# Block-sparse attention with an eight-expert router: rows of the late expert tiles turned by VectorE instead of TensorE, and one addition moved ahead in a queue

## The chip, the core and the metric

One of the eight cores of a Trainium2 chip runs the whole program. The metric is the device time of one execution in microseconds (us). Four compute engines matter: TensorE (PE in the profile; PEld is its weight load), VectorE (DVE), ScalarE (ACT) and GpSimd (POOL); SyncE (SP) issues most DMAs, GpSimd the indirect ones. Each engine works through its own queue of instructions in order and waits on semaphores where it needs the work of another.

## The reference

All data is float32. The attention has 4 sequences of 768 positions, 8 heads of 64 features, and blocks of 32 positions; the mask `mask` is set by the neighbouring, first, last and sampled blocks.

```python
scores = scale * np.matmul(q, k.transpose(0, 1, 3, 2))
scores = np.where(mask, scores, -1000000000.0)
attn = softmax(scores)
x = np.matmul(attn, v)              # then laid out as 3072 rows of 512 features

xn, en = x / |x|, expert_emb / |expert_emb|
logits = xn @ en.T / tau            # 8 experts
expert_idx = argmax(logits); gate_w = softmax(logits)[expert_idx]
for e in range(8):                  # w1[e]: 512 x 1024, w2[e]: 1024 x 512
    mask = expert_idx == e
    h = np.maximum(x[mask] @ w1[e], 0.0)
    out[mask] = gate_w[mask, None] * (h @ w2[e])
```

## The kernel before

**Attention.** A unit is 128 keys against 384 queries (half a sequence) for a pair of heads; six units make a half pair, and there are 32 half pairs. `score_fast` makes the products of keys and queries (line L358, tile `sc`) and their exponentials on ScalarE (L361, tile `e`). `attend_fast` sums the exponentials over the six units on VectorE (`esum`, L374 and L376) and multiplies by the values into one PSUM accumulator, `av` (L379), of which there is only one buffer. After the sixth unit ScalarE copies one bank of `av` (`part`, L383) and VectorE adds the other bank to it (`at`, L385); then `av` is free for the next half pair. `settle` turns `at` back to rows with TensorE (L407, L414) and divides, into `x`. Between units other work for VectorE is put in: `turn_blocks` turns the 32x32 blocks of the next pair's keys and queries (L274, `kt` and `qt`), and routing and dispatch of earlier sequences run in steps at fixed units. Steps of this kind are traced in a block `issue_after(...)`, which keeps each of their instructions behind a named instruction of the same engine.

**Routing.** `route` finds for each row the expert and the gate, stores the gate as the 513th element of the row, and SP writes the rows to DRAM: `x_dram` for all sequences, `x_early` for the first two.

**Dispatch and experts.** Five early tiles of 128 rows, each of a single expert, are cut from the first two sequences (`slot_e`), while the last sequences are still in attention. The remaining rows are ranked once all are known (`dispatch_late`, `fill_slots`), which gives `slot_l`: for each late tile and each of its 128 places the number of a row. Of 24 late tiles at most, 19 always run and the others only if they are needed (a branch each); in this execution 20 do. Two of the late tiles are mixed: two experts with 64 rows each (`mixed_tile`), placed among the others by `ORDER`.

For tile i, `expert_tile` does

- `fetch`: GpSimd gathers the rows of a later tile from DRAM into one of four buffers `xg` (L785), and SP loads the next expert's `w1` and `w2`, 2048 KB each, into a ring of three (L807). The program asks for the rows of tile i + 2; the scheduler that orders the instructions puts the gather ahead of the scatter before it, so in the compiled order the rows of tile i + 3 are gathered at the start of late tile i;
- 32 products `hp` = w1 by the turned rows `xgt` (L845), in two halves; ScalarE applies the ReLU to the first half (L848), VectorE to the second (L852);
- `prepare(i + 1)`: TensorE turns the next tile's rows with four transposes (L830, tile `xg_ps`), and VectorE copies them to `xgt` (L832);
- 8 products `yp` = h by w2 (L858);
- `finish`: VectorE multiplies by the gate (L866, tile `y`, of which there are two buffers) and GpSimd scatters the rows to the output (L867).

A product in float32 appears in the profile as two matmuls. In a mixed tile the products hold the rows as weights (L886, L906), and `h` is turned back with eight transposes (L898), between whose two halves the next tile is prepared. At the end of the program a count of good denominators decides whether an exact second version has to run; it does not here.

Of the kernel before, what the change touches and what calls it, by code (L numbers as in the profile page):

```python
# [42 lines left out]
for _mixed in range(MIX):  # L43
    ORDER.insert(6 * (_mixed + 1), _mixed)
XW = DM + 1
SCALE = 1.0 / float(D) ** 0.5
# [279 lines left out]
def attend(k, u):  # L326
    nc = k.nc
    h, c = u // NC, u % NC
    g, hh = h // 2, h % 2
    b = g // NPAIR  # L330
    et, v = k.ets.pop(u), k.vs[g]
    if c == 0:
        k.av = two_banks(k, "av")[:, 0, 0:NC * D].rearrange("p (c e) -> p c e", e=D)
    for kc in range(NC):
        nc.tensor.matmul(k.av[:, c, :], lhsT=et[:, kc * P:(kc + 1) * P], rhs=v[:, hh, kc, :],
                         start=(kc == 0), stop=(kc == NC - 1))
    if c == NC - 1:
        if h % H == 0:
            k.x[b] = k.xp.tile([P, NC, XW], F32, name="x", tag="x")
# [3 lines left out]
        at = (h % H) * D  # L343
        nc.vector.tensor_tensor(out=k.x[b][:, :, at:at + D], in0=k.av,
                                in1=den.unsqueeze(2).broadcast_to([P, NC, D]), op=ALU.mult)
# [19 lines left out]
def attend_fast(k, u):  # L365
# [15 lines left out]
    if kc == NC - 1:  # L381
        part = k.sp.tile([P, HALF], F32, name="part", tag="part")
        nc.scalar.copy(out=part, in_=k.av[:, 1, 0:HALF])  # L383
        at = k.sp.tile([P, HALF], F32, name="at", tag="at")
        nc.vector.tensor_tensor(out=at, in0=k.av[:, 0, 0:HALF], in1=part, op=ALU.add)  # L385
        k.done[u // NC] = (at, k.esum)


def settle(k, w):
# [5 lines left out]
    if w % (2 * NPAIR) == 0:  # L395
        k.x[b] = k.xp.tile([P, NC, XW], F32, name="x", tag="x")
        k.nsq[b] = k.xp.tile([P, NC, NPAIR], F32, name="nsq", tag="nsq")
# [11 lines left out]
    for t in range(NQ):  # L409
# [14 lines left out]
    nc.vector.tensor_tensor(  # L424
        out=k.x[b][:, chunks, j * P:(j + 1) * P].rearrange("p t (h d) -> p t h d", h=2),
        in0=rows[:, :, :, 0:D], in1=inv.unsqueeze(3).broadcast_to([P, NQ, 2, D]), op=ALU.mult)
# [4 lines left out]
def squares(k, w):  # L431
# [3 lines left out]
    chunks = slice(qh * NQ, (qh + 1) * NQ)  # L435
    x = k.x[b][:, chunks, j * P:(j + 1) * P]
    sq = k.sp.tile([P, NQ, P], F32, name="sq", tag="sq", bufs=1)
# [9 lines left out]
def last_squares(k, w):  # L447

    b, j, qh = w // (2 * NPAIR), w // 2 % NPAIR, w % 2
    for c in range(qh * NQ, (qh + 1) * NQ):  # L450
        sq = k.sp.tile([P, P], F32, name="sq_l", tag="sq_l")
        k.nc.scalar.activation(sq, k.x[b][:, c, j * P:(j + 1) * P], ACT.Square,
                               accum_out=k.nsq[b][:, c, j:j + 1])
# [20 lines left out]
def logits(k, x):  # L474
    nc, p = k.nc, k.rp
    lg = two_banks(k, "lg")[:, 0, 0:NC * E].rearrange("p (c e) -> p c e", e=E)
    for c2 in range(0, NC, 2):
        ps = k.big.tile([P, 2 * ND, P], F32, name="xt_ps", tag="big")
        for i in range(2 * ND):
            c, d = c2 + i // ND, i % ND  # L480
            nc.tensor.transpose(ps[:, i, :], x[:, c, d * P:(d + 1) * P], k.ident)
        xt = p.tile([P, 2 * ND, P], F32, name="xt")
# [8 lines left out]
def route(k, b):  # L491
# [3 lines left out]
    if k.exact:  # L495
        for c in range(NC):
            sq = p.tile([P, DM], F32, name="sq")
            nc.scalar.activation(sq, x[:, c, 0:DM], ACT.Square, accum_out=nrm[:, c:c + 1])
    else:
# [29 lines left out]
    nc.vector.reduce_max(out=m, in_=pick, axis=AX.X)  # L529
    nc.vector.tensor_tensor(out=oh, in0=pick, in1=wide(m), op=ALU.is_equal)  # L530
    yield
# [3 lines left out]
    for w in (4, 2):  # L535
        nc.gpsimd.tensor_tensor(out=ex[:, :, 0:w], in0=ex[:, :, 0:w], in1=ex[:, :, w:2 * w], op=ALU.add)
    gate = x[:, :, DM:XW]
    nc.gpsimd.tensor_tensor(out=gate, in0=ex[:, :, 0:1], in1=ex[:, :, 1:2], op=ALU.add)
    nc.gpsimd.tensor_scalar(out=gate, in0=gate, scalar1=1e-9, scalar2=None, op0=ALU.add)
    yield  # L540
    nc.vector.reciprocal(out=gate, in_=gate)
    yield
    drams = (k.x_early, k.x_dram) if b < EARLY else (k.x_dram,)
    for dram in drams:
        for c in range(NC):
            nc.sync.dma_start(out=dram[b * S:(b + 1) * S, :].rearrange("(c p) w -> p c w", c=NC)[:, c], in_=x[:, c])
            yield
# [91 lines left out]

def fill_slots(k, lanes, val, nt, tiles, name):  # L640

    nc, p = k.nc, k.dp
    ps = two_banks(k, "slot_ps")[:, 0, 0:2 * tiles]
    for t in range(nt):
# [46 lines left out]
def dispatch_late(k):  # L691
# [63 lines left out]
    yield  # L755
    k.slots.append(fill_slots(k, k.lanes, val, NT, NL, "slot_l"))
    yield
# [18 lines left out]
def fetch_rows(k, i):  # L776

    late = int(i >= NE)
    x = ring(k, "xg", i, 4, k.wp, [P, XW])
    t = ORDER[i - NE] if late else i  # L780
    slot = k.slots[late][:, t:t + 1]
    with ExitStack() as order:
        if k.squared is not None and not late:
            order.enter_context(k.tc.issue_after(k.squared))
        k.nc.gpsimd.indirect_dma_start(  # L785
            out=x[:, :], out_offset=None, in_=(k.x_dram if late else k.x_early)[:, :],
            in_offset=bass.IndirectOffsetOnAxis(ap=slot, axis=0),
            bounds_check=N if late else EARLY * S - 1, oob_is_err=False,
        )
    k.rows[i] = x, slot  # L790


def fetch_weights(k, i, at, pieces=1):
# [28 lines left out]
def prepare(k, i):  # L822

    x = k.rows[i][0]
    if i == 0:
        ps = two_banks(k, "first")[:, 0].rearrange("p (d t) -> p d t", d=ND)
    else:
        ps = ring(k, "xg_ps", i, 1, k.eps, [P, ND, P])
    for d in range(ND):
        k.nc.tensor.transpose(ps[:, d, :], x[:, d * P:(d + 1) * P], k.ident)  # L830
    k.turned_rows[i] = ring(k, "xgt", i, 2, k.wp, [P, ND, P])
    k.nc.vector.tensor_copy(out=k.turned_rows[i], in_=ps)  # L832


def expert_tile(k, i, meanwhile=None):
    nc = k.nc
    ((w1, w2),), (x, slot) = k.weights.pop(i), k.rows.pop(i)
    xt = k.turned_rows.pop(i)
    h = ring(k, "h", i, 2, k.wp2, [P, NF, P])
    half = NF // 2  # L840
    for f0 in (0, half):
# [9 lines left out]
        else:  # L851
            nc.vector.tensor_scalar(out=h[:, half:NF], in0=hp, scalar1=0.0, scalar2=None, op0=ALU.max)  # L852

# [3 lines left out]
    for f in range(NF):  # L857
        nc.tensor.matmul(yp, lhsT=h[:, f, :], rhs=w2[:, f, :], start=(f == 0), stop=(f == NF - 1))  # L858
    finish(k, i, yp, x, slot)


def finish(k, i, yp, x, slot):

    nc = k.nc
    y = ring(k, "y", i, 2, k.wp2, [P, DM])
    nc.vector.tensor_scalar(out=y, in0=yp, scalar1=x[:, DM:XW], scalar2=None, op0=ALU.mult)  # L866
    nc.gpsimd.indirect_dma_start(  # L867
# [5 lines left out]
def mixed_tile(k, i):  # L873


    nc = k.nc
    weights, (x, slot) = k.weights.pop(i), k.rows.pop(i)
    xt = k.turned_rows.pop(i)
    half = NF // 2
    rows = []  # L880
    for f0 in (0, half):
# [9 lines left out]
        else:  # L891
            nc.vector.tensor_scalar(out=row, in0=hp, scalar1=0.0, scalar2=None, op0=ALU.max)
        rows.append(row)
# [13 lines left out]
    finish(k, i, yp, x, slot)  # L907

# [268 lines left out]
```

## Time and profile before

| | |
|---|---|
| median of 3 runs | 712.66 us (711.72 to 712.91) |
| the profiled execution's own time | 712.75 us |
| its span in the profile | 711.0 us |
| mean granted TensorE clock | 0.994 |
| VectorE, ScalarE, GpSimd busy | 332.6, 188.5, 230.0 us |
| attention alone / both / expert tiles alone | to about 324 / to 336 / from 336 to 698 us |
| moved by DMA | 164.76 MB, mean 232 GB/s |

A row of the timeline or of the chain begins with its start and its duration in us; a row of instruction groups gives a count (x) and a mean or minimum/median/maximum in ns. A row of the waits gives the engine and line that waited, the engine and line that it waited for, the total in us, the number of waits, and the longest. In the windows each engine's busy time in a stretch is followed by the granted clock, the DMA share and the GB/s.

### The profile page before, as it was taken

How to read it: one execution, taken by the hardware profiler on the slowest of the kernel's cores; microseconds unless marked ns; L12 is line 12 of the kernel's file. 1: busy time of each engine (PE TensorE's matmuls, PEld its weight loads, DVE VectorE, ACT ScalarE, POOL GpSimd, SP SyncE). 2: the span in 40 equal slices, each digit the busy share in tenths (PEclk: the TensorE clock that was granted, in tenths of full speed). 3: DMA queues.
4: the chain of work that ended last, by engine and by line, in shares of the span. 5: the costliest groups of instructions: out<-in, count | busy, mean ns of one | idle time of the engine just before them, and what ended most of it. 6: DMA issues, size and time to landing. Idle time of an engine off the chain costs nothing.

```text
span 711.0 us, 19426 instructions
## 1 busy us (share of the span) xinstructions
PE 693.6 (98%) x8313; PEld 436.5 (61%) x8313; DVE 332.6 (47%) x684; ACT 188.5 (27%) x266; POOL 230.0 (32%) x383
## 2 busy tenths in 40 slices
PE   9999999999999999999999999999999999999992
PEld 4555555555555554557767777676676756667771
DVE  6887778777878888765661111111111111111110
ACT  5455545555555455453000000000000000000000
POOL 1255466544764367545401111112111111112010
PEclk9999999999999999999999999999999999999997
DMA  7632333575326768553999989988899998999990
GB/s 133 116 63 43 59 68 69 128 135 122 65 41 155 127 157 219 193 165 113 274 398 397 368 319 344 337 321 302 313 405 397 400 333 313 404 396 396 343 320 18
DMA packets 180808, 164.76 MB, mean 232 GB/s; under 512 B 128284, under 2 KB 128284, under 8 KB 180710
## 3 DMA queue, kind: packets, MB, share of 16 engines
q1 hardware_dynamic: 174950, 149.80, 67.1%
q0 software_dynamic: 4160, 13.39, 4.8%
q8 instruction: 69, 1.13, 0.7%
q10 hardware_dynamic: 1600, 0.20, 0.2%
q14 instruction: 29, 0.24, 0.1%
HBM read 147.62 MB, written 16.01 MB: 230 GB/s over the span
## 4 chain that ended last, share of the span: by engine, by line
PE 90%; issue 3%; DVE 3%; POOL 1%; ACT 1%; DMA 1%; POOLq 0%; DVEq 0%; SPq 0%; ACTq 0%
PE hp L845 21%; PE yp L858 21%; PE sc L358 20%; PE av L379 17%; PE back L414 3%; PE hp L886 2%; PE yp L906 2%; PE xg_ps L830 1%; PE back L407 1%; ACT e L361 1%; PE warm L80 1%; DVE kt L274 1%; DVE esum L376 1%; DVE at L385 0%; DMA out_dram<-y,slot_l 0%
## 5 line engine op out<-in xcount | busy, mean ns | idle before, releaser
L361 ACT ACTIVATE e<-sc 128x768 f32<-128x768 f32 x192 | 155.7, 811 | 154.9 <-PE sc L358 149.7
L845 PEld LDWEIGHTS hp<-xgt,w 128*128 128x128 f32 x1472 | 167.7, 192 | 10.8 <-issue 10.2
L845 PE MATMUL hp<-xgt,w 128*128 128x128 f32 x1472 | 169.1, 275 | 0.0
L858 PE MATMUL yp<-w,h 128*128 128x512 f32 x368 | 162.0, 593 | 0.1
L358 PE MATMUL sc<-qt,kt 64*64 64x384 f32 x1536 | 157.9, 482 | 0.0
L379 PE MATMUL av<-e,vld 64*64 64x384 f32 x1536 | 154.9, 487 | 3.0 <-DVE at L385 2.8
L376 DVE TENSOR_TENSOR esum<-esum,e 128x768 f32<-128x768 f32 x128 | 131.6, 1028 | 40.4 <-ACT e L361 38.6
L858 PEld LDWEIGHTS yp<-w,h 128*128 128x128 f32 x368 | 68.0, 190 | 77.5 <-issue 76.3
L442 POOL TENSOR_TENSOR sq<-sq 128x192 f32<-128x192 f32 (+1 forms) x186 | 106.0, 570 | 13.9
L867 POOL DMA_INDIRECT out_dram<-y,slot_l x20 | 20.2, 1008 | 246.0 <-DVE y L866 233.9
L848 ACT ACTIVATE h<-hp 128x512 f32<-128x512 f32 x23 | 13.7, 597 | 298.3 <-PE hp L845 298.3
L379 PEld LDWEIGHTS av<-e,vld 64*64 64x64 f32 x1536 | 53.8, 133 | 61.0 <-issue 28.2
L866 DVE TENSOR_SCALAR y<-yp,xg 128x512 f32<-128x512 f32 x25 | 18.8, 751 | 140.7 <-PE yp L858 128.2
L358 PEld LDWEIGHTS sc<-qt,kt 64*64 64x64 f32 x1536 | 58.9, 133 | 38.5 <-issue 36.2
L852 DVE TENSOR_SCALAR h<-hp 128x512 f32<-128x512 f32 x23 | 15.9, 692 | 131.6 <-PE hp L845 131.6
L438 POOL TENSOR_TENSOR sq<-x 128x384 f32<-128x384 f32 x31 | 27.1, 874 | 121.9 <-DVE part L427 101.9
L358 PE MATMUL sc<-qmask,kmask 64*64 64x384 bf16 x768 | 65.9, 323 | 0.1
L358 PEld LDWEIGHTS <-kmask 64*64 64x64 bf16 x768 | 24.7, 107 | 33.1 <-issue 33.0
L374 DVE TENSOR_TENSOR esum<-e 128x768 f32<-128x768 f32 x32 | 30.7, 959 | 10.0 <-ACT e L361 9.4
L414 PE MATMUL back<-ones,esum 64*64 64x1 f32 x1536 | 26.4, 190 | 0.0
L414 PEld LDWEIGHTS back<-ones,esum 64*64 64x64 f32 x1536 | 25.6, 135 | 0.0
L785 POOL DMA_INDIRECT xg<-x_dram,slot_l x22 | 22.6, 1027 | 6.7 <-issue 6.7
(191 smaller groups left out, 361.4 us busy)
## 6 DMA issues: line engine op xcount, KB each, us to landing
w<-in_moe_w_dram SPq DMA_DIRECT2D x54, 2048.0 KB
w<-in_moe_w_dram SPq DMA_DIRECT2D x16, 512.0 KB
x_dram<-x SPq DMA_DIRECT2D x24, 256.5 KB
vld<-in_v_dram SPq DMA_DIRECT2D x32, 192.0 KB
kld<-in_k_dram SPq DMA_DIRECT2D x60, 96.0 KB
qld<-in_q_dram SPq DMA_DIRECT2D x60, 96.0 KB
x_early<-x SPq DMA_DIRECT2D x12, 256.5 KB
ticks<-dens SPq DMA_DIRECT2D x32, 0.0 KB
```

The source lines that it names most:

```text
L358: nc.tensor.matmul(ps[D * r:D * (r + 1), h, 0:HALF], lhsT=rows[D * h:D * (h + 1), keys], rhs=cols[D * h:D * (h + 1), queries], start=first ...
L361: k.exps = nc.scalar.activation(e, ps[:, :, 0:HALF], ACT.Exp, scale=SCALE)
L374: k.summed = nc.vector.tensor_tensor(out=k.esum, in0=k.first, in1=e, op=ALU.add)
L376: k.summed = nc.vector.tensor_tensor(out=k.esum, in0=k.esum, in1=e, op=ALU.add)
L379: nc.tensor.matmul(k.av[D * h:D * (h + 1), r, 0:HALF], lhsT=v[D * r:D * (r + 1), h, kc, :], rhs=e[D * r:D * (r + 1), h, :], start=(kc == 0 ...
L414: nc.tensor.matmul(sums[D * s:D * (s + 1), t, h, r:r + 1], lhsT=esum[D * r:D * (r + 1), h, cols], rhs=k.ones[D * r:D * (r + 1), 0:1], star ...
L438: nc.gpsimd.tensor_tensor(out=sq, in0=x, in1=x, op=ALU.mult)
L442: k.squared = nc.gpsimd.tensor_tensor(out=out, in0=sq[:, :, 0:width], in1=sq[:, :, width:2 * width], op=ALU.add).ins
L785: k.nc.gpsimd.indirect_dma_start(out=x[:, :], out_offset=None, in_=(k.x_dram if late else k.x_early)[:, :], in_offset=bass.IndirectOffsetO ...
L845: nc.tensor.matmul(hp[:, f, :], lhsT=w1[:, d, (f0 + f) * P:(f0 + f + 1) * P], rhs=xt[:, d, :], start=(d == 0), stop=(d == ND - 1))
L858: nc.tensor.matmul(yp, lhsT=h[:, f, :], rhs=w2[:, f, :], start=(f == 0), stop=(f == NF - 1))
L867: nc.gpsimd.indirect_dma_start(out=k.out[:, :], out_offset=bass.IndirectOffsetOnAxis(ap=slot, axis=0), in_=y[:, :], in_offset=None, bounds ...
```

## The change

Late tiles no longer use TensorE for turning rows. A row in DRAM is now four quarters, each 128 features and a copy of the gate (129 elements, 516 in all). For a late tile four gathers fetch, for each group of 32 rows, the four quarters of these rows into four groups of 32 partitions. VectorE's transpose of 32x32 blocks, reading every fourth element, then leaves on partition p the features 4p to 4p + 3 of all rows; `w1` of late tiles is loaded in the same order of features. The indices of the quarters are made in `fill_slots` by four products with a constant `spread`, and each row's gate is picked from the gathered copies with a mask `mine` and a sum. Early tiles are turned as before. The turn of the next tile's rows is queued behind VectorE's ReLU of the present tile.

In the attention, `at` becomes the instruction that later VectorE work is queued behind: `k.summed` now names it after the sixth unit, and the first addition of a half pair is queued behind it. The reciprocal that makes the gate is queued behind the choice of expert.

```diff
-XW = DM + 1
+XE = P + 1
+XW = ND * XE
 # build_consts
+    groups = k.ident.rearrange("p (g t) -> p g t", g=NG)
+    k.spread = pool.tile([P, NG, NG, BLK], F32, name="spread")
+    nc.vector.tensor_copy(out=k.spread, in_=groups.unsqueeze(2).broadcast_to([P, NG, NG, BLK]))
+    k.mine = pool.tile([P, NG], F32, name="mine")
+    nc.vector.reduce_sum(out=k.mine, in_=groups, axis=AX.X)
+    no = iota(k, "group_no", [P, NG], [[1, NG]])
+    k.group = pool.tile([P, 1], F32, name="group")
+    nc.vector.tensor_tensor(out=no, in0=no, in1=k.mine, op=ALU.mult)
+    nc.vector.reduce_sum(out=k.group, in_=no, axis=AX.X)
 # attend_fast
     elif kc == 1:
         k.esum = k.sp.tile([P, 2, HALF], F32, name="esum", tag="esum")
-        k.summed = nc.vector.tensor_tensor(out=k.esum, in0=k.first, in1=e, op=ALU.add)
+        with k.tc.issue_after(k.summed.ins if u > NC else k.exps.ins):
+            k.summed = nc.vector.tensor_tensor(out=k.esum, in0=k.first, in1=e, op=ALU.add)
...
-        nc.vector.tensor_tensor(out=at, in0=k.av[:, 0, 0:HALF], in1=part, op=ALU.add)
+        k.summed = nc.vector.tensor_tensor(out=at, in0=k.av[:, 0, 0:HALF], in1=part, op=ALU.add)
 # route
-    nc.vector.reciprocal(out=gate, in_=gate)
+    with k.tc.issue_after(picked):
+        nc.vector.reciprocal(out=x[:, :, :, P], in_=gate.broadcast_to([P, NC, ND]))
 # fill_slots
-    nc.vector.tensor_scalar(out=slot, in0=got, scalar1=0.0, scalar2=None, op0=ALU.max)
+    nc.vector.tensor_scalar(out=got, in0=got, scalar1=0.0, scalar2=None, op0=ALU.max)
+    nc.vector.tensor_copy(out=slot, in_=got)
+    if not quarters:
+        return slot
+    ps = both[:, 1, 0:NG * tiles].rearrange("p (g t) -> p g t", g=NG)
+    for g in range(NG):
+        nc.tensor.matmul(ps[:, g], lhsT=k.spread[:, g].rearrange("p e t -> p (e t)"), rhs=got, start=True, stop=True)
+    k.quarter = k.const.tile([P, NG, tiles], I32, name="quarter")
+    nc.vector.tensor_scalar(out=k.quarter, in0=ps, scalar1=float(ND), scalar2=k.group[:, 0:1], op0=ALU.mult,
+                            op1=ALU.add)
 # fetch_rows, late tiles
+            quarters = k.x_dram.rearrange("n (e w) -> (n e) w", e=ND)
+            for g in range(NG):
+                k.nc.gpsimd.indirect_dma_start(
+                    out=x[:, g], out_offset=None, in_=quarters,
+                    in_offset=bass.IndirectOffsetOnAxis(ap=k.quarter[:, g, t:t + 1], axis=0),
+                    bounds_check=quarters.shape[0] - 1, oob_is_err=False,
+                )
 # fetch_weights
-        src = src[bass.ds(e, 1), :, :].rearrange("o (c p) f -> p (o c) f", p=P)
+        order = "o (p c) f -> p (o c) f" if w is w1 and i >= NE else "o (c p) f -> p (o c) f"
+        src = src[bass.ds(e, 1), :, :].rearrange(order, p=P)
 # prepare, late tiles (early tiles keep the transposes of TensorE)
+    with k.tc.issue_after(k.relu):
+        nc.vector.transpose(out=turned.rearrange("p d (g t) -> p d g t", g=NG),
+                            in_=x[:, :, 0:P].rearrange("p g (t d) -> p d g t", d=ND))
+        own = ring(k, "own", i, 2, k.wp, [P, NG])
+        nc.vector.tensor_tensor(out=own, in0=x[:, :, P], in1=k.mine, op=ALU.mult)
+        gate = ring(k, "gate", i, 3, k.wp, [P, 1])
+        nc.vector.reduce_sum(out=gate, in_=own, axis=AX.X)
 # finish
-    nc.vector.tensor_scalar(out=y, in0=yp, scalar1=x[:, DM:XW], scalar2=None, op0=ALU.mult)
+    nc.vector.tensor_scalar(out=y, in0=yp, scalar1=gate, scalar2=None, op0=ALU.mult)
```

More of the change, by code (lines that the diff above doesn't have):

```diff
@@ L338, in attend @@
         if h % H == 0:
-            k.x[b] = k.xp.tile([P, NC, XW], F32, name="x", tag="x")
+            k.x[b] = k.xp.tile([P, NC, ND, XE], F32, name="x", tag="x")
         den = k.sums.pop(h)
@@ L342, in attend @@
         nc.vector.reciprocal(out=den, in_=den)
-        at = (h % H) * D
-        nc.vector.tensor_tensor(out=k.x[b][:, :, at:at + D], in0=k.av,
+        nc.vector.tensor_tensor(out=k.x[b][:, :, h % H // 2, D * hh:D * (hh + 1)], in0=k.av,
                                 in1=den.unsqueeze(2).broadcast_to([P, NC, D]), op=ALU.mult)
@@ L395, in settle @@
     if w % (2 * NPAIR) == 0:
-        k.x[b] = k.xp.tile([P, NC, XW], F32, name="x", tag="x")
+        k.x[b] = k.xp.tile([P, NC, ND, XE], F32, name="x", tag="x")
         k.nsq[b] = k.xp.tile([P, NC, NPAIR], F32, name="nsq", tag="nsq")
@@ L424, in settle @@
     nc.vector.tensor_tensor(
-        out=k.x[b][:, chunks, j * P:(j + 1) * P].rearrange("p t (h d) -> p t h d", h=2),
+        out=k.x[b][:, chunks, j, 0:P].rearrange("p t (h d) -> p t h d", h=2),
         in0=rows[:, :, :, 0:D], in1=inv.unsqueeze(3).broadcast_to([P, NQ, 2, D]), op=ALU.mult)
@@ L435, in squares @@
     chunks = slice(qh * NQ, (qh + 1) * NQ)
-    x = k.x[b][:, chunks, j * P:(j + 1) * P]
+    x = k.x[b][:, chunks, j, 0:P]
     sq = k.sp.tile([P, NQ, P], F32, name="sq", tag="sq", bufs=1)
@@ L451, in last_squares @@
         sq = k.sp.tile([P, P], F32, name="sq_l", tag="sq_l")
-        k.nc.scalar.activation(sq, k.x[b][:, c, j * P:(j + 1) * P], ACT.Square,
+        k.nc.scalar.activation(sq, k.x[b][:, c, j, 0:P], ACT.Square,
                                accum_out=k.nsq[b][:, c, j:j + 1])
@@ L480, in logits @@
             c, d = c2 + i // ND, i % ND
-            nc.tensor.transpose(ps[:, i, :], x[:, c, d * P:(d + 1) * P], k.ident)
+            nc.tensor.transpose(ps[:, i, :], x[:, c, d, 0:P], k.ident)
         xt = p.tile([P, 2 * ND, P], F32, name="xt")
@@ L496, in route @@
         for c in range(NC):
-            sq = p.tile([P, DM], F32, name="sq")
-            nc.scalar.activation(sq, x[:, c, 0:DM], ACT.Square, accum_out=nrm[:, c:c + 1])
+            sq = p.tile([P, ND, P], F32, name="sq")
+            nc.scalar.activation(sq, x[:, c, :, 0:P], ACT.Square, accum_out=nrm[:, c:c + 1])
     else:
@@ L529, in route @@
     nc.vector.reduce_max(out=m, in_=pick, axis=AX.X)
-    nc.vector.tensor_tensor(out=oh, in0=pick, in1=wide(m), op=ALU.is_equal)
+    picked = nc.vector.tensor_tensor(out=oh, in0=pick, in1=wide(m), op=ALU.is_equal).ins
     yield
@@ L536, in route @@
         nc.gpsimd.tensor_tensor(out=ex[:, :, 0:w], in0=ex[:, :, 0:w], in1=ex[:, :, w:2 * w], op=ALU.add)
-    gate = x[:, :, DM:XW]
+    gate = p.tile([P, NC, 1], F32, name="gate")
     nc.gpsimd.tensor_tensor(out=gate, in0=ex[:, :, 0:1], in1=ex[:, :, 1:2], op=ALU.add)
@@ L545, in route @@
         for c in range(NC):
-            nc.sync.dma_start(out=dram[b * S:(b + 1) * S, :].rearrange("(c p) w -> p c w", c=NC)[:, c], in_=x[:, c])
+            nc.sync.dma_start(out=dram[b * S:(b + 1) * S, :].rearrange("(c p) w -> p c w", c=NC)[:, c],
+                              in_=x[:, c].rearrange("p e w -> p (e w)"))
             yield
@@ L637, in split_lanes, with fill_slots @@
         yield
-def fill_slots(k, lanes, val, nt, tiles, name):
+def fill_slots(k, lanes, val, nt, tiles, name, quarters=False):
     nc, p = k.nc, k.dp
-    ps = two_banks(k, "slot_ps")[:, 0, 0:2 * tiles]
+    both = two_banks(k, "slot_ps")
+    ps = both[:, 0, 0:2 * tiles]
     for t in range(nt):
@@ L755, in dispatch_late @@
     yield
-    k.slots.append(fill_slots(k, k.lanes, val, NT, NL, "slot_l"))
+    k.slots.append(fill_slots(k, k.lanes, val, NT, NL, "slot_l", True))
     yield
@@ L778, in fetch_rows @@
     late = int(i >= NE)
-    x = ring(k, "xg", i, 4, k.wp, [P, XW])
+    x = ring(k, "xg", i, 4, k.wp, [P, ND, XE])
     t = ORDER[i - NE] if late else i
@@ L784, in fetch_rows @@
             order.enter_context(k.tc.issue_after(k.squared))
[L785 to L789, printed above, removed]
+        if late:
+            quarters = k.x_dram.rearrange("n (e w) -> (n e) w", e=ND)
[5 more added lines that the diff above has]
+                )
+        else:
+            k.nc.gpsimd.indirect_dma_start(
+                out=x.rearrange("p e w -> p (e w)"), out_offset=None, in_=k.x_early[:, :],
+                in_offset=bass.IndirectOffsetOnAxis(ap=slot, axis=0), bounds_check=EARLY * S - 1, oob_is_err=False,
+            )
     k.rows[i] = x, slot
@@ L822, in prepare @@
 def prepare(k, i):
[L824 to L832, printed above, removed]
+    nc = k.nc
+    x, slot = k.rows[i]
+    turned = k.turned_rows[i] = ring(k, "xgt", i, 2, k.wp, [P, ND, P])
+    if i < NE:
+        if i == 0:
+            ps = two_banks(k, "first")[:, 0].rearrange("p (d t) -> p d t", d=ND)
+        else:
+            ps = ring(k, "xg_ps", i, 1, k.eps, [P, ND, P])
+        for d in range(ND):
+            nc.tensor.transpose(ps[:, d, :], x[:, d, 0:P], k.ident)
+        nc.vector.tensor_copy(out=turned, in_=ps)
+        k.rows[i] = x[:, 0, P:XE], slot
+        return
+    with k.tc.issue_after(k.relu):
[5 more added lines that the diff above has]
+        nc.vector.reduce_sum(out=gate, in_=own, axis=AX.X)
+    k.rows[i] = gate, slot
 def expert_tile(k, i, meanwhile=None):
     nc = k.nc
-    ((w1, w2),), (x, slot) = k.weights.pop(i), k.rows.pop(i)
+    ((w1, w2),), (gate, slot) = k.weights.pop(i), k.rows.pop(i)
     xt = k.turned_rows.pop(i)
@@ L851, in expert_tile @@
         else:
-            nc.vector.tensor_scalar(out=h[:, half:NF], in0=hp, scalar1=0.0, scalar2=None, op0=ALU.max)
+            k.relu = nc.vector.tensor_scalar(out=h[:, half:NF], in0=hp, scalar1=0.0, scalar2=None, op0=ALU.max).ins
     if i + 1 < NE + NL:
@@ L858, in expert_tile, with finish @@
         nc.tensor.matmul(yp, lhsT=h[:, f, :], rhs=w2[:, f, :], start=(f == 0), stop=(f == NF - 1))
-    finish(k, i, yp, x, slot)
-def finish(k, i, yp, x, slot):
+    finish(k, i, yp, gate, slot)
+def finish(k, i, yp, gate, slot):
     nc = k.nc
     y = ring(k, "y", i, 2, k.wp2, [P, DM])
-    nc.vector.tensor_scalar(out=y, in0=yp, scalar1=x[:, DM:XW], scalar2=None, op0=ALU.mult)
+    nc.vector.tensor_scalar(out=y, in0=yp, scalar1=gate, scalar2=None, op0=ALU.mult)
     nc.gpsimd.indirect_dma_start(
@@ L876, in mixed_tile @@
     nc = k.nc
-    weights, (x, slot) = k.weights.pop(i), k.rows.pop(i)
+    weights, (gate, slot) = k.weights.pop(i), k.rows.pop(i)
     xt = k.turned_rows.pop(i)
@@ L891, in mixed_tile @@
         else:
-            nc.vector.tensor_scalar(out=row, in0=hp, scalar1=0.0, scalar2=None, op0=ALU.max)
+            k.relu = nc.vector.tensor_scalar(out=row, in0=hp, scalar1=0.0, scalar2=None, op0=ALU.max).ins
         rows.append(row)
@@ L906, in mixed_tile @@
             nc.tensor.matmul(yp[lanes, :], lhsT=h[:, f, lanes], rhs=w2[:, f, :], start=(f == 0), stop=(f == NF - 1))
-    finish(k, i, yp, x, slot)
+    finish(k, i, yp, gate, slot)
 def after_sequence(n, b):
```

## The prediction

> **What bounds the kernel now.** I read the page first, engine shares and slices, then the table of windows, then the chain of work by time, then the timeline around two places.
>
> ```profile
> PE 693.6 (98%) x8313; PEld 436.5 (61%) x8313; DVE 332.6 (47%) x684; ACT 188.5 (27%) x266; POOL 230.0 (32%) x383
> PEclk9999999999999999999999999999999999999997
> ...
> 428.13 0.44 PE xg_ps L830 x4
> 428.57 6.87 PE yp L858 x16
> 435.44 7.14 PE hp L845 x64
> 442.58 0.44 PE xg_ps L830 x4
> 443.02 6.87 PE yp L858 x16
> ```
>
> TensorE is busy for 98% of the span at full clock, so only what leaves its queue, or what it waits for, can move the end. In the late expert stage the chain has no gap: a tile is 7.14 us of first products, 0.44 us of four transposes of the next tile's rows, 6.87 us of second products, 14.45 us together. Two places are touched: this stage, and the boundaries between half pairs in the attention. Three lines of the latter, and what TensorE waits for in the whole span:
>
> ```profile
> 48.00 1.02 DVE L274 STREAM_TRANSPOSE kt<-kld 128x384 f32<-128x384 f32 x2
> 48.00 0.47 ACT L383 COPY part<-av 128x384 f32<-128x384 f32 x1
> 48.95 0.51 DVE L385 TENSOR_TENSOR at<-av,part 128x384 f32<-128x384 f32 x1
> 49.52 1.52 PE L379 MATMUL av<-e,vld 64*64 64x384 f32 x16
> ...
> PE av L379 <- DVE at L385: 2.8, 7, 0.7
> ```
>
> The addition `at` frees the only accumulator `av`. Its input `part` is ready at 48.47, but two transposes of the next pair's keys stand ahead of it on VectorE, so it runs at 48.95 and the next `av` products start at 49.52.
>
> **The change, part by part.** *Transposes of late rows.* Per late tile `prepare` drops four TensorE transposes and the eviction `xgt` (0.68 us, VectorE). Tiles 5 to 24 and the unused tile 25, prepared within the last, make 21. In 19 of them the whole 0.44 us is on the path: 19 x 0.44 = 8.4 us. In two the following tile is prepared inside a mixed tile (lines L886 to L906), where those 0.44 us cover VectorE's `row`: it ends at 501.02 (500.33 + 0.69) while the first four transposes of `row` end at about 500.68; the second four would start 0.06 us sooner than at 501.11, say 0.1 us gained. So 2 x 0.1 = 0.2. Together **8.6 us**. `yp` can start at once, since its first half of `h` comes from ScalarE, done 3 us before; the second half is needed four products (1.7 us) into `yp`, and VectorE's L852 delivers it 0.75 us after `hp` ends.
>
> *What replaces them.* VectorE turns 128x512 in one instruction, then multiplies 128x4 and reduces to one gate. The row for `kt`, 0.55 us for 384 elements, gives 0.73 us for 512; the small two are 0.2 us each by rows such as L733 and L560 (0.15 to 0.16). They stand behind L852 in the queue and end about 1.9 us after `hp`; the turned rows are needed by the next tile's `hp`, 6.9 us after. Behind them waits `y`, which is not ready before then. So they cost nothing; without that cover they would cost 1.1 us x 20. But the read now steps by four floats, which no row shows. The Trainium skill ("SBUF — State Buffer", section Door 1, the note on cachelines) speaks against this: an access that goes to a new 16-byte line each time pays a penalty, and a step of four floats does so at every element. It gives no size. By the row the sum is 0; if the penalty made it three times slower, 2.2 us, it is still 0, since only above 0.73 + 5.0 = 5.7 us does `hp` wait. I take 0; ends 0 and, at ten times slower (7.3 us), 1.6 x 20 = 32 us lost. A gain is excluded: nothing waits for VectorE here.
>
> *Gathers.* One gather of 128 rows of 2052 bytes becomes four of 516 bytes, each issued from POOL.
>
> ```profile
> L785 POOL DMA_INDIRECT xg<-x_dram,slot_l x22: 1019/1024/1053, 379.0 to 686.0; - x22
> DMA to landing us min/median/max: 5.3/7.5/11.1
> 422.05 1.01 POOL L867 DMA_INDIRECT out_dram<-y,slot_l  x1 [12.11 <-DVE y L866]
> 423.38 1.03 POOL L785 DMA_INDIRECT xg<-x_dram,slot_l  x1 [0.31 <-issue]
> 436.50 1.01 POOL L867 DMA_INDIRECT out_dram<-y,slot_l  x1 [12.10 <-DVE y L866]
> ```
>
> With the 0.3 us between them a gather holds POOL 1.33 us; four and the scatter make 6.6 us of a 14.0 us tile, so POOL still waits for `y`. The scatter behind them is `y` of the present tile, later anyway. In the order of instructions before and after, the gather at the start of tile i is for tile i+3, read in the middle of i+2: 2 x 14.0 + 7.1 = 35 us, less 5.3 us of issue and 11 us of landing, leaves 19 us. The first late tile has least: indices at about 378.7, four gathers until 384.2, landed by 395 at the latest, read at 399.3. There the scheduler also puts 3 + 3 gathers for tiles 7 and 8 ahead of the scatter of tile 3, which goes some 4 us late; its buffer `y` is next written by tile 5, at 421. Cost 0. The skill speaks against the quarters too ("DMA: Bandwidth & Descriptors", How a descriptor splits into AXI transactions): a descriptor not starting on 256 bytes reads from the boundary below. At a pitch of 516 bytes, four quarters are by my estimate 84 beats against 69 for one row, 25% of 0.26 MB, 0.2 us of transfer a tile. The windows say there is room:
>
> ```profile
> 450.00:500.00 50.00, 50.00 (x283) 33.62 (x282) 6.79 (x10) 2.39 (x4) 8.14 (x8) 1.00 0.87 317
> 600.00:650.00 50.00, 50.00 (x299) 37.32 (x298) 7.40 (x11) 2.39 (x4) 6.25 (x7) 1.00 1.03 396
> SPq L807 <- PE yp L858: 114.5, 21, 6.7
> ```
>
> The last columns are DMA share and GB/s. A tile moves 4.72 MB (two weights of 2048 KB, rows in 256.5, rows out 256), 327 GB/s at 14.45 us and 337 at 14.01; after a mixed tile, which takes two sets, the engines catch up at 396. SP's issues wait for TensorE to free buffers, not for the engines. By the row and by the rule alike 0; with the rule 4.92/14.01 = 351 GB/s, below 396. If that cover were gone, the 0.2 us would count 20 times, 4 us.
>
> *Order of w1.* Per partition four pieces of 4 KB become one of 16 KB. The row is the same 2048 KB load; none shows 16 KB pieces. I take 0. A gain is excluded by SP waiting for TensorE; the loss is a rival below.
>
> *Indices.* `fill_slots` adds, for the late call, two VectorE instructions (0.18 us each), four fp32 products of 128x24 and one read of them. The nearest row is the product `good_ps` a little later: from 377.84 to the next `hp` at 378.06, 0.22 us. Four: **+0.9 us** on TensorE. They stand four `hp` groups (0.89 us) behind the slot products, so at 377.94, and `got` is ready at 377.9: no wait. `good_ps` needs the same bank and stands 0.67 us later; the read takes 0.18.
>
> *Constants, gate column.* Four VectorE instructions (about 1.2 us by the copy and reduce rows) come in at 6.8 us, where VectorE idles 0.91 us before `kt` and 1.05 before `esum`; `kt`'s second half is then 0.3 us later and read at 12.5. Cost 0; without cover 1.2. The reciprocal over 24 instead of 6 elements and rows of 2064 instead of 2052 bytes: 0.6% more of 9 MB, SP has time; 0.
>
> *Additions first.* `at` now heads VectorE's queue, ahead of the `kt` transposes and of dispatch work at all such boundaries. `part` is ready 1.0 us before the scores end, `at` takes 0.55, so TensorE should find `av` free, as it does at boundaries without transposes: there sixteen `av` products take 1.29 us, here 1.52. In the chain 11 stretches have 1.52 and three 1.42 to 1.50: 11 x 0.23 + 0.5 = 3.0 us, besides the 2.8 us of waits, 5.8 at most. VectorE loses up to 0.4 us at each by waiting for `part`, and transposes and `esum` follow later: the keys are a whole half pair early, but where routing fills VectorE to 9 tenths some comes back. No row shows that; ends -5.8 and +1, I take **-4.8**, near the counted waits. What is late next there is ScalarE's exponential for want of a free `e`.
>
> **Sum.** -8.6 + 0.9 - 4.8 = -12.5 us. The profiled execution took 712.75 us (span 711.0, 1.75 around it), 0.09 above the median of 712.66. 712.75 - 12.5 = 700.25; against the median **700.2 us**.
>
> **Rivals.** *Tiles only:* the reordering gives nothing, because the wait moves from `at` to `esum` and the exponentials; VectorE at 8 to 9 tenths of the slices up to 320 us speaks for it, TensorE's whole wait list of 2.8 us for little at stake. 712.7 - 8.6 + 0.9 = 705.0.
>
> *Attention only:* a late gather or a slow turn takes back the 0.44 us of each tile. For it: nothing measured of quarters. Against: 19 and 5 us of slack. 712.7 - 4.8 + 0.9 = 708.8.
>
> *Slower: DMA becomes the bound through w1.* The share is already 0.87 to 1.03. At 396 GB/s the other 2.62 MB of a set take 6.6 us, leaving 7.4 us of 14.01 for w1's 2.10 MB: from 283 GB/s down TensorE falls behind. 22 sets are read in the stage and some 14 us are held ahead, so the gain of 12.5 is eaten from (12.5 + 14)/22 = 1.2 us a set, 244 GB/s. At 220 GB/s it is 9.5 us, 2.1 x 22 - 14 - 12.5 = +20: 733 us. Against it: 4 KB pieces reach 396, and longer ones read the same bytes in a straighter order.
>
> *The change does not do what it says:* the same count of TensorE instructions. The order of the changed kernel shows the transposes gone; only balance of gain and loss leaves it within 0.2%.
>
> **Numbers.** Forecast 0.66; tiles only 0.14; attention only 0.05; balance 0.04; slower 0.11 (w1 0.06, the turn or the gathers far beyond their bounds 0.05). Faster 0.85, same 0.04, slower 0.11, with 0.2%, 1.4 us, about what a measurement here can tell. The forecast alone spans 697.0 (full 8.8 and 5.8, less 0.9, and 2 us that I don't see) to 704; with tiles only the range goes to 706, and the two hold 0.80.
>
> **What would show it.** Chain: `hp` x64 followed by `yp` x16 with nothing between, period 14.0. Turn near 0.73 us, ended 5 us before the next `hp`. Four gathers of 1.0 us each. No TensorE wait for `at`; 1.29 us at the boundaries. Wrong: a TensorE wait for w1 or for the turned rows, or a period still near 14.4; or `esum` and the exponentials on the chain more often than now.

## The result, and the profile after

The changed kernel takes 702.23 us (median of 4 runs, 701.82 to 702.70) where the kernel before takes 712.78 (4 runs): ratio 0.9858, 95% interval 0.9843 to 0.9873, so 10.5 us less. The forecast was 700.2, with a range of 697 to 706. The profiled execution took 701.82, its span is 700.1 (before: 712.75 and 711.0).

The page of the changed kernel, shares and slices:

```profile
PE 683.5 (98%) x8237; PEld 449.7 (64%) x8237; DVE 345.2 (49%) x733; ACT 188.4 (27%) x266; POOL 296.3 (42%) x450
PEclk9999999999999999999999999999999999999997
```

TensorE has 76 instructions and 10 us of work less and is still busy for 98%. GpSimd has 66 us more work. The chain of work in the middle of the late stage, and one boundary of half pairs:

```profile
418.97 7.14 PE hp L891 x64
426.12 6.87 PE yp L904 x16
432.99 7.14 PE hp L891 x64
440.13 6.87 PE yp L904 x16
...
58.62 1.29 PE av L390 x16
```

`hp` is followed by `yp` with nothing between; a tile takes 14.01 us where it took 14.45. In the whole chain of the attention 30 of the 31 stretches of sixteen `av` products last 1.29 us and one 1.32; none has the 1.52 of before. What TensorE still waits for is new:

```profile
PE hp L891 <- issue: 2.0, 2, 1.0
PE yp L904 <- DVE h L898: 1.2, 2, 0.9
PE hp L944 <- DVE row L938: 0.5, 2, 0.2
```

Apart from 0.3 us of the second row, the first two rows belong to one place, tiles 3 and 4, just after the indices of the quarters are ready. The chain there:

```profile
372.41 0.85 PE slot_ps L672 x8
...
374.32 9.54 another core or an unknown queue
...
383.88 0.70 DVE h L898
...
384.63 3.70 PE yp L904 x8
388.33 3.02 PE hp L891 x25
391.35 1.04 issue
392.39 0.47 PE hp L891 x2
392.86 0.94 issue
393.80 4.29 PE hp L891 x37
398.09 6.87 PE yp L904 x16
404.96 7.14 PE hp L891 x64
```

The first row is the one foreseen cost, the products with `spread`. Below it the chain loses its thread for 9.54 us: it finds no instruction that released `h`. The timeline of the same stretch tells what was under way:

```profile
379.15 0.99 POOL L812 DMA_INDIRECT xg<-x_dram,quarter  x1 [0.30 <-DMA out_dram<-y,slot_e]
379.66 0.60 PE L867 MATMUL xg_ps<-ident,xg 128*128 128x128 f32 x4
380.09 3.60 PE L904 MATMUL yp<-w,h 128*128 128x512 f32 x8
...
383.88 14.59 SPq L841 DMA_DIRECT2D w<-in_moe_w_dram  x3
383.88 0.69 DVE L898 TENSOR_SCALAR h<-hp 128x512 f32<-128x512 f32 x1 [9.56 <-remote]
384.36 1.00 POOL L812 DMA_INDIRECT xg<-x_dram,quarter  x1 [0.30 <-issue]
```

TensorE is done with `hp` of tile 3 by 379.7, since `xg_ps` follows it. VectorE's ReLU `h` starts 4.2 us after that, and SP's load of weights, which waits for the same products, in the same instant. Meanwhile GpSimd issues gathers with 0.30 us between them: fourteen in a row from 373.89 to 391.86, for tiles 5 and 6 whole and three quarters each of 7 and 8. Where the time went, by the chains of before and after:

| stretch | before | after | difference |
|---|---|---|---|
| start to the slot products (`slot_ps`, 24) | 376.61 | 370.82 | -5.8 |
| from there to `hp` of tile 5 | 29.93 | 34.14 | +4.2 |
| from there to the start of the last scatter | 292.58 | 284.72 | -7.9 |
| from there to the end of the span | 11.88 | 10.42 | -1.5 |

### The profile page after: what moved, and what is told of

The parts are those of the page before. It is cut to its first block, busy times and chain, and to the rows that moved or that the text cites. A ratio compares the mean times of both kernels' runs of the same rounds, so it can differ in the third digit from the quotient of the medians.

```text
span 700.1 us, 19413 instructions
## 1 busy us (share of the span) xinstructions
PE 683.5 (98%) x8237; PEld 449.7 (64%) x8237; DVE 345.2 (49%) x733; ACT 188.4 (27%) x266; POOL 296.3 (42%) x450
## 4 chain that ended last, share of the span: by engine, by line
PE 93%; issue 2%; another core or an unknown queue 1%; DVE 1%; POOL 1%; ACT 0%; POOLq 0%
PE sc L368 22%; PE hp L891 21%; PE yp L904 21%; PE av L390 18%; PE back L425 3%; PE hp L932 2%; PE yp L952 2%; PE back L418 2%; PE warm L81 1%; POOL xg L812 0%; DVE row L938 0%; POOL nrm L514 0%; PE hp L944 0%; DVE h L898 0%
## 5 line engine op out<-in xcount | busy, mean ns | idle before, releaser
L368 PE MATMUL sc<-qt,kt 64*64 64x384 f32 x1536 | 162.7, 482 | 0.0
L390 PE MATMUL av<-e,vld 64*64 64x384 f32 x1536 | 158.9, 486 | 0.0
L812 POOL DMA_INDIRECT xg<-x_dram,quarter x88 | 88.2, 1003 | 140.4 <-DVE gate L877 101.5
L387 DVE TENSOR_TENSOR esum<-esum,e 128x768 f32<-128x768 f32 x128 | 129.3, 1010 | 34.4 <-ACT e L371 30.6
L453 POOL TENSOR_TENSOR sq<-sq 128x192 f32<-128x192 f32 (+1 forms) x186 | 103.3, 555 | 13.9
L390 PEld LDWEIGHTS av<-e,vld 64*64 64x64 f32 x1536 | 62.4, 133 | 47.2 <-issue 18.2
L368 PEld LDWEIGHTS sc<-qt,kt 64*64 64x64 f32 x1536 | 65.2, 133 | 32.3 <-issue 25.1
L368 PE MATMUL sc<-qmask,kmask 64*64 64x384 bf16 x768 | 71.6, 323 | 0.1
L912 DVE TENSOR_SCALAR y<-yp,gate 128x512 f32<-128x512 f32 x20 | 15.0, 751 | 101.0 <-PE yp L904 88.8
L368 PEld LDWEIGHTS <-kmask 64*64 64x64 bf16 x768 | 30.3, 107 | 27.4 <-issue 23.1
```

The lines of the kernel that those rows point to most:

```text
L368: nc.tensor.matmul(ps[D * r:D * (r + 1), h, 0:HALF], lhsT=rows[D * h:D * (h + 1), keys], rhs=cols[D * h:D * (h + 1), queries], start=first ...
L390: nc.tensor.matmul(k.av[D * h:D * (h + 1), r, 0:HALF], lhsT=v[D * r:D * (r + 1), h, kc, :], rhs=e[D * r:D * (r + 1), h, :], start=(kc == 0 ...
L453: k.squared = nc.gpsimd.tensor_tensor(out=out, in0=sq[:, :, 0:width], in1=sq[:, :, width:2 * width], op=ALU.add).ins
L812: k.nc.gpsimd.indirect_dma_start(out=x[:, g], out_offset=None, in_=quarters, in_offset=bass.IndirectOffsetOnAxis(ap=k.quarter[:, g, t:t + ...
```

## The experiments

**The parts alone.** a_reorder is the kernel before with the first of these edits, b_tiles the changed kernel without it:

```diff
-        k.summed = nc.vector.tensor_tensor(out=k.esum, in0=k.first, in1=e, op=ALU.add)
+        with k.tc.issue_after(k.summed.ins if u > NC else k.exps.ins):
+            k.summed = nc.vector.tensor_tensor(out=k.esum, in0=k.first, in1=e, op=ALU.add)
...
-        nc.vector.tensor_tensor(out=at, in0=k.av[:, 0, 0:HALF], in1=part, op=ALU.add)
+        k.summed = nc.vector.tensor_tensor(out=at, in0=k.av[:, 0, 0:HALF], in1=part, op=ALU.add)
```

> The kernel before with the reordering of the attention alone: at is what later VectorE work is queued behind, and the first addition of a half pair is queued behind it; rows, w1 and the turn stay as before. Theory: the reordering gives what the two traces show between the first and the last boundary, 5.9 us, so about 706.8 us, with av boundaries of 1.29 us and no wait of TensorE for at. Rival: part of the 5.9 us comes from the dispatch or the constants, which the change altered too; then 708 to 710 us. Rival of the record (the wait moves to esum and the exponentials): about 712.7 us.

> The changed kernel without the reordering of the attention. Theory: the tiles give 8.0 us up to the last product, the indices cost 0.9 us and the stretch of tiles 3 and 4 some 4 us, so about 708 us (4.5 us under before). If the parts don't add (VectorE's queue in the attention decides what the dispatch gives), it lies above 709 or below 706.5 us.

Against 712.92 us of before on that chip, a_reorder took 707.41 (ratio 0.9926, 0.9909 to 0.9942) and b_tiles 708.16 (0.9930, 0.9914 to 0.9947): 5.5 and 4.8 us, 10.3 together, where both at once gave 10.5. The parts add. The last boundary of the attention stands in the chain at 322.48 before and at 317.15 in a_reorder, 5.3 us earlier, and nothing of it is given back: the slot products start at 371.25 where they started at 376.61. b_tiles too starts them a little earlier, at 375.94, so some 0.5 us of the 5.8 in the table above are not the reordering's; what they are wasn't pursued. TensorE's waits in b_tiles show the old wait for `at` and the new ones side by side:

```profile
PE av L389 <- DVE at L395: 1.9, 5, 0.7
PE hp L890 <- issue: 1.7, 5, 0.4
PE yp L903 <- DVE h L897: 1.5, 2, 1.1
```

**The stretch of tiles 3 and 4.** Two suspects: the fourteen gathers, and the 16 KB pieces of w1. c_behind keeps each late gather behind the scatter of the tile before; d_pieces loads late w1 in four transfers of 4 KB a partition.

```diff
 # c_behind, fetch_rows (k.scattered is the scatter in finish)
+        if late and k.scattered is not None and i < NE + NU + 2:
+            order.enter_context(k.tc.issue_after(k.scattered))
 # d_pieces, fetch_weights
-        step = w.shape[1] // pieces
+        step = w.shape[1] // (ND if w is w1 and i >= NE else pieces)
```

> The changed kernel with the gathers of each late tile queued on GpSimd behind the scatter of the tile before, so that no more than four gathers stand in a row where there were fourteen (span 374 to 392 us). Theory 1, the burst of fourteen gathers is what delays others in tiles 3 and 4: the 4 us lost there come back, about 698.3 us, and TensorE waits neither for h nor for issue there. Theory 2, the 16 KB packets of w1 delay the weights or the events: no change, 702.2 us. Theory 3, the gathers' packets themselves, wherever they stand: the loss is spread over more tiles, 700 to 702 us.

> The changed kernel with each late w1 loaded in four transfers of 4 KB a partition in place of one of 16 KB; the order of features is unchanged. Theory 1 (the burst of gathers costs the 4 us): no change, 702.2 us, and the same stalls in tiles 3 and 4. Theory 2 (the 16 KB packets do): the stalls of tiles 3 and 4 shrink, 698 to 700 us. Against both: three more issues of SP for each w1 could come late behind its waits, 703 us or more.

c_behind took 699.80 us (0.9819, 0.9802 to 0.9835), d_pieces 703.33 (0.9869, 0.9853 to 0.9886). In d_pieces the gap of the chain is still there, 11.08 us long. In c_behind, with four gathers and then a scatter that waits for `y`, the chain has no gap:

```profile
373.77 5.69 PE hp L893 x50
379.46 0.44 PE xg_ps L869 x4
379.90 6.87 PE yp L906 x16
386.77 7.14 PE hp L893 x64
393.91 6.87 PE yp L906 x16
400.78 7.14 PE hp L893 x64
```

From the slot products (370.46) to `hp` of tile 5 it takes 30.32 us, against 34.14 in the changed kernel: in these two executions the row of gathers costs 3.8 us. The last scatter starts at 685.51, 4.2 us earlier than in the changed kernel. The time fell by 2.4 us only, because what follows that start took 12.3 us instead of 10.4; no engine has work there. Both were run again side by side:

> The changed kernel once more, beside c_again on the same chip: 702.2 us, with tile 5 beginning some 4 us later than in c_again.

> The kernel c_behind once more, to be read against after_again. If the row of gathers costs the stretch of tiles 3 and 4 what the chains say (4.2 us), the difference is 4.2 us less whatever the end of the program gives or takes (1.9 us more in the first pair of profiles): 2 to 4 us, 698 to 700 us.

The changed kernel took 702.70 us (0.9861, 0.9845 to 0.9876), c_behind 699.48 (0.9816, 0.9802 to 0.9829), 3.2 us apart. In the profiles of this pair the same stretch takes 37.10 us in the changed kernel (an execution of 705.17 us, the slowest of its four) and 30.31 in c_again: there the row costs 6.8 us, a fallen clock included (0.68 from 396 to 402 us). In d_pieces it takes 35.28. So fourteen gathers have no fixed price; 3.8 us is the least of the profiled executions. By its time, c_behind beats both kernels.

**A row of gathers elsewhere.** To separate the row from its place, e_row16 and e_row10 are c_behind with twelve and six more gathers of quarters behind the four of tile 14, early in tile 12, into places that nobody reads. f_spaced puts small multiplications on GpSimd between groups of four; f_small gathers 43 elements a row instead of 129.

```diff
 # fetch_rows, behind the four gathers
+            if i == 14:
+                for r in range(12):          # 6 in e_row10
+                    k.nc.gpsimd.indirect_dma_start(out=(spare if r % 2 else used)[:, r // 2 % 3], ...
 # f_spaced, ahead of each fourth of these
+                        for _ in range(5):
+                            with k.tc.issue_after(last):
+                                last = k.nc.gpsimd.tensor_tensor(out=idle, in0=idle, in1=idle, op=ALU.mult).ins
```

> The kernel c_behind (699.8 us) with twelve more gathers of the same quarters, into spare places that nobody reads, right behind the four gathers of one tile in the middle of the late stage: sixteen gathers in a row at another place than tiles 3 and 4. Theory 1 (many gathers in a row delay the events of other engines, wherever it is): 3 to 5 us lost there, about 704 us, with TensorE waiting for h and hp stalling as in tiles 3 and 4 of the changed kernel. Theory 2 (the loss belongs to the place: first use of late rows, the first 16 KB loads, good and its branch): no loss, 699.8 us. Theory 3 (GpSimd is merely late with the scatter): y comes free late, which the two buffers cover; 699.8 to 701 us with a wait of DVE y for the scatter.

> As e_row16 with six more gathers: ten in a row. If the loss grows with each gather in a row, about half of that of e_row16, 701.5 to 702 us; if only more than eight outstanding gathers matter, less; if the place decides, 699.8 us.

> e_row16 (710.5 us against 699.8 of c_behind) with the sixteen gathers in groups of four: five small GpSimd multiplications of 128x125 elements, about 1.7 us together by the 0.82 us of the 128x384 row, stand between the groups. Nobody reads what the twelve extra gathers bring. Theory 1 (the unbroken row starves the events of other engines, a pause lets them through): most of the 10.7 us come back, 700 to 703 us. Theory 2 (the number of gathers outstanding or queued counts): still 708 to 711 us. If GpSimd is merely late, the gathers of the next tile come up to 5 us late, and that much would be lost with a wait of DVE for the rows.

> e_row16 with the twelve extra gathers bringing 43 instead of 129 elements a row (172 instead of 516 bytes), the number of rows and of instructions unchanged; nobody reads them. If the bytes count, the loss of 10.7 us shrinks to a third, about 703 us; if the gather instructions or their 128 rows count, it stays, 709 to 711 us.

| kernel | gathers in a row | median us | over 699.8 |
|---|---|---|---|
| e_row10 | 10 | 701.18 | 1.4 |
| e_row16 | 16 | 710.53 | 10.7 |
| f_small, short rows | 16 | 709.84 | 10.0 |
| f_spaced | 4 x 4 | 700.46 | 0.7 |

Neither the place nor the bytes decide, and the number of gathers alone doesn't either: sixteen with pauses cost next to nothing. It is the unbroken row that costs, and between ten and sixteen its price rises from 1.4 to 10.7 us. The 95% intervals of e_row10 and f_spaced overlap that of c_behind; for e_row10 the trace shows the loss too, one wait of 1.3 us of TensorE for `h`. The timeline of e_row16 in tiles 12 and 13:

```profile
508.48 3.60 PE L915 MATMUL yp<-w,h 128*128 128x512 f32 x8
508.93 0.99 POOL L823 DMA_INDIRECT spread<-x_dram,quarter  x1 [0.30 <-issue]
...
512.63 0.69 DVE L909 TENSOR_SCALAR h<-hp 128x512 f32<-128x512 f32 x1 [10.51 <-remote]
...
521.20 0.27 PE L902 MATMUL hp<-xgt,w 128*128 128x128 f32 x1 [1.75 <-issue]
521.93 0.27 PE L902 MATMUL hp<-xgt,w 128*128 128x128 f32 x1 [0.46 <-issue]
```

and the same stretch of f_spaced:

```profile
507.10 1.00 POOL L814 DMA_INDIRECT xg<-x_dram,quarter  x1 [0.30 <-issue]
507.94 7.03 PE L922 MATMUL yp<-w,h 128*128 128x512 f32 x16
508.13 2.29 POOL L828 TENSOR_TENSOR spread<-spread 128x125 f32<-128x125 f32 x5
509.22 0.69 DVE L916 TENSOR_SCALAR h<-hp 128x512 f32<-128x512 f32 x1 [7.63 <-PE hp L909]
```

`h` follows the start of `yp` by 4.15 us in the row and by 1.28 us where GpSimd pauses after the fourth gather, 1.1 us after that gather's end. So the news of a finished product reaches VectorE late while the row goes on. A pause does two things, though. In f_spaced the gathers' DMA queue also runs dry (no packet of it between 520 and 522 us), while in e_row16 it has packets all the way from 507 to 529. Whether the issuing or the queue that never empties delays the others was not separated. In e_row16 TensorE's own matmuls then come singly with gaps that the profile calls issue (5.2 us in 7 waits), and the granted clock falls, as the windows show:

```profile
500.00:515.00 15.00, 13.70 (x84) 9.59 (x79) 2.65 (x5) 0.60 (x1) 9.85 (x10) 1.00 0.83 306
515.00:525.00 10.00, 5.93 (x30) 4.26 (x29) 0.00 (x0) 0.00 (x0) 7.10 (x8) 0.86 1.03 381
525.00:535.00 10.00, 8.82 (x42) 7.79 (x43) 1.78 (x3) 0.60 (x1) 5.02 (x5) 0.63 0.96 354
```

Part of the 10.7 us is therefore the clock after the stall (0.63 in the third row), not the stall: the last 37 matmuls of this `hp` take 7.01 us in the chain, where 37/64 of 7.14 is 4.1. Through what the gathers hold up the others isn't settled: for the late instructions the profile finds no releaser (`remote`). A late load of instructions is not what it shows: no packet of the instruction queues lies between 507 and 527 us of e_row16. The expectation for e_row16, 704 us, was 6.5 us too low.

**The price of the transposes, and the cover of the turn.** Both are c_behind with one thing more: t_idle has TensorE's four transposes back, read by nobody; v_five has VectorE's turn five times over.

```diff
 # t_idle, prepare of late tiles
+    ps = ring(k, "xg_ps", i, 1, k.eps, [P, ND, P])
+    for d in range(ND):
+        nc.tensor.transpose(ps[:, d, :], x[:, d, 0:P], k.ident)
 # v_five, around the turn
+        for _ in range(5 if len(parts(i - 1)) == 1 else 1):
```

> The kernel c_behind (699.8 us) with the four TensorE transposes of each late tile put back where they stood; nobody reads their result, VectorE still turns the rows. It prices the transposes alone. Theory (their whole duration was on TensorE's path): 18 to 19 x 0.44 us, so 8.0 to 8.6 us more, about 708 us. Rival (part of them was hidden, and the gain came from elsewhere, such as VectorE's shorter queue): less than 6 us more, under 706 us.

> The kernel c_behind (699.8 us) with VectorE's turn of 1.09 us done five times over instead of once, except where the present tile is mixed. Theory (the turn has about 5 us to spare before hp needs the rows): it ends 0.75 + 5.45 = 6.2 us after hp, 0.7 us before the next hp, so no change, 699.8 us. Rival (the cover is smaller because y, own and gate stand behind it): up to 1 us a tile, 705 to 715 us.

t_idle took 706.62 us (0.9914, 0.9897 to 0.9930), 6.8 more than c_behind, between the two expectations. The chains decide: from the slot products to the last scatter it is 323.33 us against 315.05, 8.28 more, close to 19 x 0.44. In the two mixed tiles the time is the same, so there the transposes were wholly hidden:

```profile
494.75 0.59 PE hp L949 x4
495.34 0.44 PE xg_ps L875 x4
495.77 0.45 PE hp L949 x4
```

They last 1.48 us; in c_behind the same place has 0.59, a gap of 0.23 and 0.66, also 1.48. The missing 1.5 us lie again after the start of the last scatter, 10.7 us here.

v_five took 708.60 us (0.9943, 0.9927 to 0.9960), 8.8 more: my expectation failed.

```profile
PE hp L894 <- DVE xgt L875: 4.5, 16, 0.6
...
409.47 0.69 DVE L901 TENSOR_SCALAR h<-hp 128x512 f32<-128x512 f32 x1 [7.60 <-PE hp L894]
```

The first row is TensorE's wait for the turned rows, the second the ReLU of tile 5 in the timeline. I had let it start 0.05 us after `hp` ends. In c_behind's order the four gathers end in just that moment (here at 408.41), and `h` starts 1.0 us after the end of `hp` (408.43, as its 7.14 us began at 401.29): ReLU and five turns of 1.10 us then end at 415.7, after `yp` (415.3), and the period is 14.47 instead of 14.01. The rival was right, with another cause than it gave: not what stands behind the turn, but the late start ahead of it.

## Why the prediction was right, and where its steps were off

The sum was -12.5 us; the path to the last scatter lost 9.4, the end of the program another 1.5. Both main terms worked by the mechanism that was named. That the total still came within 2 us is in part luck: a cost of 3.8 us was left out, and two gains paid for most of it: 1.0 us more before the slot products than the sum took, and 1.5 us at the end of the program that it did not have.

*Transposes of late rows: right.* Predicted -8.6 (19 x 0.44 and 2 x 0.1). The stretch from tile 5 on gives -7.9 for 18 tiles, and 0.44 is gained in tile 4: -8.3. t_idle puts the same price on them. The 0.1 in each mixed tile was not there: the second half waits 0.2 us for `row` (PE hp L944 above), as the transposes had filled that time.

*The turn: right in being hidden, wrong in its duration.* 0.73 us was predicted from `kt`; it is 1.09:

```profile
L872 DVE STREAM_TRANSPOSE xgt<-xg 128x512 f32<-128x512 f32 x21 | 22.9, 1093 | 0.0
L285 DVE STREAM_TRANSPOSE kt<-kld 128x384 f32<-128x384 f32 x32 | 16.6, 554 | 2.1 <-DMA kld<-in_k_dram 1.4 <-DMA emb<-in_moe_expert_emb_dram 0.7
```

That is 2.13 ns an element (1093/512) against 1.44 (554/384), 1.5 times as long. The note on cachelines of the Trainium skill ("SBUF — State Buffer", Door 1) has the right direction with its penalty for each new line, and the size is measured here. Its next sentence counts a stride of 4 fp32 as free; if that means a step of four, the measured 1.5 times speaks against it. Whether the step alone makes the difference was not separated from what else differs between the two rows. In the changed kernel `h` starts at 398.13 and the turn ends at 399.82, 5.1 us before the next `hp`: the room of 5 us was right there. In this kernel the gathers wait for `gate`, which follows the turn, so they start 2 us after `h`:

```profile
426.15 0.69 DVE L898 TENSOR_SCALAR h<-hp 128x512 f32<-128x512 f32 x1 [6.39 <-PE hp L891]
...
428.17 1.02 POOL L812 DMA_INDIRECT xg<-x_dram,quarter  x1 [7.12 <-DVE gate L877]
```

In c_behind's order they come before `h`, which starts 1.0 to 1.3 us after `hp`, and the room is that much less, which v_five found.

*Gathers: price right, cost wrong. This is the step that failed.* Each takes 1.00 us, as predicted, and the data is in time. I had seen that gathers for tiles 7 and 8 go ahead of the scatter of tile 3, and charged that only with a late scatter: "Cost 0". I asked whether GpSimd had time, not what a row of fourteen does to others. It cost 3.8 us in the profiled execution and 6.8 in that of after_again, shown by c_behind and c_again, and a row at another place cost time too, as e_row16 and f_spaced show. The order of instructions showed the row before the run; its price stood in no row of the profile. One sum of this part is off without consequence: 25% of 0.26 MB is 0.07 MB, so with the rule a tile would move 4.79 MB, 342 GB/s, and not 4.92 and 351. No run here shows that cost by itself.

*Order of w1: right at 0.* d_pieces, with 4 KB a partition, gained nothing (703.33 against 702.23). The windows of 600 to 650 us show the engines of the changed kernel at 406 GB/s with the long pieces, 396 before; the slower rival's 244 GB/s is far away:

```profile
600.00:650.00 50.00, 50.00 (x284) 36.05 (x283) 8.70 (x16) 1.79 (x3) 15.78 (x16) 1.00 1.02 406
```

*Indices: right.* 0.85 us, predicted 0.9.

*Additions first: right, a little small.* Predicted -4.8 with ends -5.8 and +1. a_reorder gives 5.5 by its time and 5.3 by its chain: nearly the whole of the boundaries and of the waits. I held back 1 us for `esum` and the exponentials becoming late, and that didn't come.

*What I left out.* From the start of the last scatter to the end of the span it took 11.9 us before, 10.4 after, and 10.4 to 12.3 in the other kernels, with no work on any engine. The same kernel once more gives 10.9 (after_again, against 10.4) and 11.9 (c_again, against 12.3), so a part of the 1.5 us gained there can be chance. In the last 7 us of the changed kernel, when the scatter has landed, the only DMA packets are five of the instruction queues; before, three in the last 8.5 us. Whether the end waits for these loads isn't shown. The gain was not foreseen and paid for part of the gathers.

## What to carry to other kernels

When one transfer becomes four, count not only the issuing engine's time but also how many the scheduler will put in an unbroken row once a common input becomes ready; look for that in the order of instructions, and tie such a row to something that pauses it. Four indirect gathers at a time cost nothing on the path here; fourteen cost 3.8 us in one execution and 6.8 in another, on engines that had nothing to do with them. And measure the cover of hidden work in the order that will run: moving the gathers took over 1 us of the turn's cover without touching VectorE.

## What the runs showed of the hardware that I had not expected

An unbroken row of GpSimd's indirect DMAs delays other engines: VectorE's and SP's release by TensorE came about 4 us late in the rows of ten and sixteen (e_row10, e_row16), VectorE's 2 to 6 us late in those of fourteen (2.1 in after_again, 4.2 in the changed kernel's first profile, 5.8 in d_pieces), and about 1 us late right behind four. It depends on the row and not on the bytes (172 or 516 bytes for each of the 128 places: 709.84 and 710.53 us), and five multiplications, 2.3 us together, between groups of four remove nearly all of it. After such a stall the granted clock can fall, to 0.63 for 10 us in e_row16; in the profiled run of after_again it was 0.68 from 396 to 402 us, in that of the first run 1.00 throughout the same stretch.
